# Another written-down order of the same operations, written-down buffer slots, and a small buffer for the last 160 tokens' piece of batch 3

## The chip, the cores and the metric

The kernel runs on one core of a Trainium2 chip. The metric is the device time of one execution in microseconds (us). The kernel before takes 217.79 us, the median of three runs (217.53 to 218.53).

A core has five engines, each with an instruction queue of its own that is worked off in order: TensorE (PE) multiplies matrices, VectorE (DVE), ScalarE (ACT) and GpSimd (POOL) work on vectors, and SyncE (SP) issues DMAs. ACT and POOL issue some DMAs too. In the profile, "PEld" is TensorE's loading of weights, "SPq" the DMA issue of SP. An engine waits for another's result on a semaphore.

## The reference

Polysketch attention, and then a token mixer on its output:

```python
# 4 batches, 4 heads, 1088 tokens, head size 32, r = 8
phi(x) = outer(S1 x, S2 x)                     # 64 features for each token
kv  = einsum('bhsf,bhsd->bhfd', phi(k), v)
z   = sum(phi(k), over s)
num = einsum('bhsf,bhfd->bhsd', phi(q), kv)
den = einsum('bhsf,bhf->bhs', phi(q), z) + 1e-6
x   = (num / den) as (batch, 1088, 4*32)

theta = x @ w_theta                            # 128x128
zr, zi = x * cos(theta), x * sin(theta)
y = w_tok_r @ zr + w_tok_i @ zi                # 1088x1088 each, over the tokens
u = x + y
out = u + relu(u @ w_ch)                       # 128x128
```

The weights come as 64-bit floats; the kernel itself turns the words of each weight into 32-bit floats.

## The kernel before, in words

**Recorded, then issued in a written order.** The kernel body computes nothing at first. Each call of `L.op(engine, duration, function, writes, reads)` in class `Layout` (L180) records one operation, with its engine ("P", "V", "A", "G", "S" for PE, DVE, ACT, POOL, SP), its buffers, and what it depends on. There are 1,020 operations. `L.run()` (L248) then walks the constant `ORDER` (L34), a permutation of their numbers, beside `STARTS`, a planned start for each in hundredths of a us. Each buffer has a class with a fixed number of slots; the first operation that touches a buffer gives it, of the free slots of its class, the one that falls free first by the planned times. `L.issue()` (L269) emits the operations in that order. Since each engine works its queue in order, `ORDER` decides what stands ahead of what on each engine, and which buffer's last use a slot has to wait for.

The classes (L344 and on) are `big` (22 slots of 1152 words for each partition: q, k, v, the converted token rows), `zs` (5 of 2176: raw token rows, turned x, z), `hf` (6 of 576), `g3` (5 of 768), `g1` (6 of 384), `sm` (13 of 192), `lv` (1) and `ps` (the 8 banks of PSUM).

**Fills.** Between two marked PE operations, `issue` also writes matmuls on a buffer of zeros (`spin`, L427, 128x384 in bf16) into PE's queue, as many as five for each planned microsecond of gap. Before them all stand 39 narrow ones (128x112). Their result is not read. There are 28 of the wide kind in the trace, one of them an operation of its own.

**Stages.** For each batch:

- `load` (L655): k, q and v, 576 KB each. k of batches 0 and 1 is issued by ACT, the rest by SP. q of batch 3 comes in four pieces of many small packets.
- key sums, grid and rests (L677 to L765) make the key features; for batches 1 to 3, `join` (L391) lets POOL issue a DMA that accumulates a correction into a second copy of k, loaded by SP at L714 ("kh" below is that copy).
- `kfeatures` (L767), `chain` (L835), `chain_out` (L933): transposes, features, the kv products, then small matrices that `levels` needs. Parts of them are POOL's (`blocks_m`, L569; masks, L379).
- `query_scale`, `query_slices` (L985, L1007), `levels` (L1033), `den` (L1059): the query features and the denominator.
- `outputs_x` (L1088): numerator, theta, sine and cosine, and the products zr and zi. For batches 1 to 3 x is transposed by a trip through DRAM: DVE transposes in blocks (L1160), SP stores it to the buffer `far` (L1161), four DMAs of SP fetch it (L1165).

**The token weights.** `weight` (L636) makes one row block of `w_tok` (there are 17, rows 0 to 16, each 1,088 KB for both w_tok_r and w_tok_i): SP loads it raw into a `zs` slot (L642), ACT converts the high words (L643) and the low words (L645), DVE shifts (L383) and adds (L379). The queue of SP, the two conversions of ACT and the two of DVE stand in order among all else that these engines do.

**The mixer.** For batches 0 and 1, `mix_row` (L1256) accumulates over the 17 row blocks in PSUM, batch 0 for three column groups together, batch 1 group by group. Batches 2 and 3 together use Winograd's seven products (`winograd`, L1352): each of m1 to m7 multiplies 544 tokens by 544 in two parts, 384 and 160 columns wide, and each result is added to u (`acc`, L1405). The number pair after "out" or "m" below is batch, half, part: out3_0_1 is batch 3's first half, the part 160 wide.

**The end.** When a piece of u is complete, `finish` (L1282) does its product with w_ch (PE), adds the relu (DVE, L386), transposes (DVE, L1303) and stores (L1299, by SP, ACT and POOL). For out3_0_1 `finish_turned` (L1329) does it in another way: PE transposes u (L1337), ACT copies that from PSUM (L1338) into `xT[3]`, the batch's own buffer, PE does the two products, DVE adds, SP and ACT store (L1347). The transposes, the copy and the products are one recorded operation.

Of the kernel before, what the change touches and what calls it, by code (L numbers as in the profile page):

```python
# [22 lines left out]
P = 128  # L23
# [11 lines left out]
    29, 32, 4, 2, 5, 0, 1, 3, 34, 30, 356, 50, 33, 102, 44, 96, 6, 108, 103, 36, 7, 51, 366, 54, 144, 8, 97, 10, 9,  # L35
    11, 55, 109, 20, 52, 12, 57, 139, 58, 59, 60, 61, 62, 63, 126, 13, 31, 132, 56, 98, 127, 264, 14, 391, 128, 143,
    245, 15, 145, 64, 65, 67, 68, 78, 35, 69, 16, 70, 19, 148, 149, 150, 151, 152, 268, 99, 66, 79, 246, 53, 80, 100,
    110, 129, 17, 133, 130, 357, 25, 361, 81, 270, 83, 18, 203, 358, 359, 71, 41, 153, 104, 271, 210, 197, 351, 257,
    45, 146, 72, 198, 73, 204, 247, 43, 258, 84, 26, 105, 360, 240, 74, 154, 323, 248, 214, 75, 82, 27, 325, 368, 106,
    155, 269, 28, 47, 76, 249, 111, 46, 77, 147, 386, 216, 85, 326, 86, 21, 327, 324, 87, 112, 205, 88, 328, 241, 89,  # L40
    120, 48, 242, 90, 206, 329, 121, 251, 367, 91, 330, 92, 134, 93, 101, 376, 392, 94, 122, 140, 252, 156, 107, 123,
    141, 369, 135, 259, 169, 142, 124, 95, 439, 436, 157, 22, 136, 362, 437, 115, 442, 217, 438, 443, 174, 440, 260,
    370, 444, 335, 441, 158, 159, 160, 161, 343, 363, 445, 265, 243, 170, 113, 446, 171, 371, 162, 352, 172, 215, 447,
    163, 164, 165, 166, 211, 39, 191, 167, 173, 448, 114, 168, 212, 175, 244, 449, 331, 176, 192, 177, 266, 450, 336,
    117, 37, 451, 341, 267, 332, 116, 253, 118, 452, 342, 339, 353, 178, 333, 272, 453, 193, 364, 340, 119, 199, 179,
    454, 125, 254, 462, 344, 387, 219, 131, 455, 137, 463, 200, 465, 180, 365, 464, 456, 181, 194, 466, 49, 458, 457,
    182, 469, 467, 459, 334, 183, 354, 460, 468, 337, 184, 470, 461, 472, 255, 138, 476, 381, 471, 473, 42, 185, 484,
    388, 474, 478, 396, 338, 273, 372, 220, 221, 274, 275, 250, 186, 40, 276, 222, 277, 256, 542, 479, 475, 539, 486,
    374, 492, 23, 373, 38, 487, 477, 195, 540, 494, 188, 480, 543, 495, 481, 355, 536, 482, 485, 218, 537, 544, 483,
    541, 278, 213, 279, 223, 280, 281, 283, 187, 224, 225, 284, 488, 226, 285, 227, 286, 287, 389, 288, 289, 290, 291,  # L50
    501, 489, 375, 538, 490, 378, 545, 502, 491, 292, 496, 261, 382, 546, 503, 498, 390, 393, 504, 547, 383, 401, 384,
    377, 548, 416, 394, 505, 549, 282, 398, 406, 379, 493, 550, 229, 380, 397, 230, 231, 262, 232, 233, 234, 235, 293,
    236, 385, 497, 237, 189, 426, 506, 304, 294, 551, 499, 238, 228, 302, 295, 552, 507, 296, 402, 303, 399, 553, 299,
    263, 403, 508, 395, 417, 418, 554, 500, 509, 555, 421, 408, 207, 558, 556, 201, 196, 239, 300, 400, 202, 301, 208,
    305, 562, 510, 559, 411, 209, 190, 557, 306, 569, 307, 560, 404, 407, 565, 308, 570, 405, 309, 561, 566, 572, 310,
    563, 345, 573, 311, 511, 564, 409, 312, 571, 313, 574, 346, 567, 314, 670, 568, 419, 676, 575, 579, 413, 316, 576,
    593, 580, 671, 412, 24, 581, 677, 577, 410, 673, 431, 678, 674, 582, 297, 586, 672, 414, 422, 512, 415, 594, 587,
    424, 578, 423, 513, 420, 427, 425, 514, 428, 429, 584, 595, 515, 583, 430, 596, 298, 675, 588, 320, 516, 679, 589,
    585, 590, 315, 598, 680, 591, 601, 624, 347, 647, 625, 681, 348, 648, 682, 649, 597, 592, 432, 626, 683, 602, 433,
    684, 603, 685, 627, 686, 604, 434, 650, 349, 317, 651, 599, 605, 687, 652, 435, 653, 654, 688, 655, 696, 628, 517,  # L60
    689, 703, 606, 350, 524, 741, 518, 738, 530, 318, 739, 690, 531, 742, 740, 319, 704, 735, 525, 743, 736, 697, 519,
    705, 737, 744, 607, 706, 745, 707, 608, 708, 709, 746, 629, 747, 656, 748, 630, 321, 749, 698, 750, 751, 609, 699,
    700, 752, 631, 701, 702, 322, 720, 753, 691, 761, 721, 754, 610, 692, 693, 657, 694, 853, 695, 632, 755, 611, 762,
    756, 722, 658, 710, 757, 758, 713, 759, 760, 763, 768, 711, 612, 764, 769, 714, 765, 659, 723, 715, 766, 782, 860,
    767, 770, 858, 775, 633, 771, 712, 772, 526, 773, 716, 774, 634, 776, 635, 789, 777, 613, 778, 660, 614, 790, 779,
    636, 717, 725, 615, 718, 780, 637, 783, 719, 616, 724, 520, 726, 727, 600, 661, 784, 728, 662, 729, 804, 781, 521,
    638, 791, 854, 813, 805, 796, 806, 797, 532, 785, 798, 792, 814, 527, 807, 730, 859, 794, 822, 786, 522, 815, 787,
    533, 816, 855, 823, 799, 793, 788, 663, 732, 639, 731, 850, 808, 800, 879, 640, 528, 861, 795, 529, 641, 832, 664,
    862, 851, 801, 833, 733, 834, 817, 523, 803, 818, 809, 857, 863, 856, 870, 534, 824, 802, 535, 944, 882, 835, 825,
    949, 948, 836, 871, 852, 819, 872, 883, 810, 884, 864, 909, 811, 865, 908, 866, 873, 874, 642, 867, 885, 875, 812,  # L70
    876, 911, 826, 820, 868, 665, 821, 890, 880, 887, 837, 838, 881, 617, 734, 891, 869, 618, 888, 899, 827, 886, 892,
    986, 900, 913, 839, 945, 840, 666, 893, 619, 894, 910, 901, 877, 946, 902, 889, 916, 952, 895, 878, 828, 829, 951,
    903, 917, 954, 904, 896, 918, 956, 897, 926, 912, 830, 919, 914, 831, 920, 898, 905, 947, 842, 953, 921, 843, 906,
    915, 927, 959, 907, 643, 958, 968, 969, 644, 922, 955, 667, 970, 841, 923, 845, 957, 960, 846, 961, 668, 950, 669,
    962, 645, 963, 971, 964, 965, 966, 972, 620, 967, 928, 985, 929, 621, 977, 844, 988, 987, 978, 989, 847, 622, 990,
    849, 848, 991, 623, 992, 973, 974, 975, 993, 646, 976, 994, 979, 930, 931, 980, 995, 981, 996, 924, 997, 998, 999,
    982, 925, 1000, 984, 983, 1008, 1001, 936, 1009, 1002, 1003, 937, 1004, 1005, 1010, 1006, 932, 1012, 1011, 933,
    1013, 1007, 934, 938, 1014, 935, 1015, 939, 1016, 1017, 1018, 940, 1019, 941, 942, 943,
)
STARTS = (  # L80
    73, 73, 90, 92, 103, 130, 170, 220, 358, 404, 449, 458, 493, 510, 538, 546, 566, 579, 580, 584, 594, 612, 628,
    666, 802, 678, 693, 694, 706, 716, 719, 732, 752, 771, 798, 811, 812, 813, 815, 817, 819, 821, 823, 838, 830, 944,
    871, 899, 904, 918, 957, 967, 1088, 998, 1026, 1061, 1064, 1066, 1111, 1113, 1115, 1129, 1129, 1408, 1142, 1145,
    1155, 1164, 1168, 1170, 1172, 1174, 1176, 1225, 1236, 1251, 1251, 1260, 1271, 1299, 1303, 1313, 1319, 1327, 1334,
    1390, 1418, 1439, 1550, 1477, 1505, 1527, 1550, 1562, 1579, 1585, 1612, 1716, 1671, 1686, 1687, 1689, 1749, 1858,
    1782, 1796, 1814, 1832, 1831, 1845, 1870, 1884, 2128, 1909, 1941, 1947, 1948, 1951, 1963, 2024, 2038, 2053, 2070,
    2073, 2103, 2093, 2101, 2129, 2138, 2153, 2179, 2272, 2187, 2240, 2248, 2261, 2278, 2293, 2293, 2304, 2414, 2348,
    2351, 2373, 2388, 2390, 2434, 2422, 2432, 2446, 2467, 2471, 2523, 2530, 2537, 2545, 2565, 2573, 2578, 2593, 2594,
    2616, 2651, 2655, 2668, 2678, 2691, 2706, 2765, 2786, 2779, 2785, 2805, 2831, 2894, 2895, 2926, 2928, 2934, 2949,
    2953, 2967, 2982, 2981, 3002, 3018, 3042, 3046, 3086, 3088, 3102, 3105, 3108, 3126, 3164, 3190, 3192, 3220, 3230,  # L90
    3267, 3296, 3319, 3321, 3342, 3360, 3390, 3410, 3417, 3424, 3430, 3450, 3437, 3451, 3483, 3488, 3498, 3530, 3516,
    3547, 3561, 3562, 3567, 3583, 3606, 3611, 3613, 3619, 3626, 3633, 3652, 3651, 3667, 3677, 3687, 3690, 3697, 3717,
    3714, 3727, 3732, 3739, 3756, 3754, 3776, 3806, 3815, 3817, 3833, 3852, 3844, 3866, 3866, 3868, 3881, 3884, 3899,
# [44 lines left out]
    21022, 21031, 21057, 21092, 21092, 21100, 21114, 21135, 21171, 21188,  # L138
)
WARM = 0  # L140
FILL = 5.0
LOAD_LEAD = 60.0
RAW_LEAD = 30.0
CHAINS = ((0,), (1,), (2, 3))
# [35 lines left out]
class Layout:  # L180
# [67 lines left out]
    def run(self):  # L248
        slots = {c: [[0.0, None] for _ in range(n)] for c, (n, _) in self.classes.items()}
        for b in self.bufs:  # L250
            b.left = len(b.ops)
# [52 lines left out]
def act(n):  # L304
    return 0.17 + 0.00083 * n
# [1238 lines left out]
```

## Time and profile before

| | |
|---|---|
| median of three runs | 217.79 us (217.53 to 218.53) |
| the profiled execution's span | 215.9 us, 1.9 below the median |
| granted TensorE clock | 1.00 in nearly every stretch |
| mean HBM traffic over the span | 157 GB/s |
| 128x384 fills; 128x112 spins | 28; 39 |
| token rows loaded | 17, 1,088 KB each |
| accumulating DMAs of POOL (L393) | issued at 21.78, 39.89 and 54.21 us |
| the kernel's first token-mix matmul row | starts at 57.2 us |

Times in the profile are microseconds from the start of the span. A group of instructions is given by its line, engine and operation, then "output<-inputs" by buffer name, then its shape, its busy time, and the idle time of that engine just before it with what ended it. The chain of waits goes back from the last instruction of the program, at each step to the thing that released it. A "share of DMA" above 1.00 means that all 16 DMA engines were busy for the whole stretch.

### The profile page before, as it was taken

How to read it: one execution, taken by the hardware profiler on the slowest of the kernel's cores; microseconds unless marked ns; L12 is line 12 of the kernel's file. 1: busy time of each engine (PE TensorE's matmuls, PEld its weight loads, DVE VectorE, ACT ScalarE, POOL GpSimd, SP SyncE). 2: the span in 40 equal slices, each digit the busy share in tenths (PEclk: the TensorE clock that was granted, in tenths of full speed). 3: DMA queues.
4: the chain of work that ended last, by engine and by line, in shares of the span. 5: the costliest groups of instructions: out<-in, count | busy, mean ns of one | idle time of the engine just before them, and what ended most of it. 6: DMA issues, size and time to landing. Idle time of an engine off the chain costs nothing.

```text
span 215.9 us, 5832 instructions
## 1 busy us (share of the span) xinstructions
PE 208.9 (97%) x2396; PEld 152.8 (71%) x2396; DVE 174.3 (81%) x343; ACT 114.5 (53%) x256; POOL 59.7 (28%) x105
## 2 busy tenths in 40 slices
PE   7899999999999999999999999999999999999992
PEld 7677798868866666866668666667677776666781
DVE  1799998999999998999999798885994747456263
ACT  4899989999998895798704233363810000000000
POOL 1272740306400000604004100000006489950403
PEclk9999999999999999999999999999999999999998
DMA  6999999995998993192002402424050420010735
GB/s 222 395 418 419 384 365 420 425 315 97 360 285 267 416 432 145 75 308 45 0 0 32 74 3 112 114 109 112 2 88 15 67 39 0 0 23 8 125 55 103
DMA packets 28046, 37.09 MB, mean 172 GB/s; under 512 B 20564, under 2 KB 23044, under 8 KB 25844
## 3 DMA queue, kind: packets, MB, share of 16 engines
q1 hardware_dynamic: 22868, 31.86, 42.4%
q0 software_dynamic: 1552, 3.25, 7.2%
q10 hardware_dynamic: 3600, 1.62, 2.8%
q8 instruction: 19, 0.31, 0.6%
q14 instruction: 7, 0.06, 0.1%
HBM read 29.84 MB, written 4.00 MB: 157 GB/s over the span
## 4 chain that ended last, share of the span: by engine, by line
PE 63%; DMA 18%; ACT 14%; issue 2%; SPq 1%; DVE 1%; POOL 1%; POOLq 0%; ACTq 0%
PE ps L399 61%; DMA zs<-w_tok 13%; DMA big<-k_l 5%; ACT big L645 4%; ACT big L643 3%; ACT lv L1056 1%; PE ps L1131 1%; ACT big L1021 1%; ACT g L1199 1%; ACT g L1202 1%; ACT g L1205 1%; ACT g L1203 1%; POOL out L1299 1%; SPq L671 0%; ACT g L1135 0%
## 5 line engine op out<-in xcount | busy, mean ns | idle before, releaser
L399 PE MATMUL ps<-big,zs 128*128 128x384 f32 (+2 forms) x380 | 110.5, 436 | 0.0
L399 PEld LDWEIGHTS ps<-big,zs 128*128 128x128 f32 x380 | 66.9, 190 | 32.5
L379 POOL TENSOR_TENSOR big<-big,big 128x544 f32<-128x544 f32 x16 | 22.1, 1458 | 48.6 <-DVE big L379 44.6
L399 PE MATMUL ps<-big,big 128*32 128x32 f32 (+2 forms) x352 | 22.8, 234 | 0.0
L643 ACT ACTIVATE big<-zs 128x1088 f32<-128x1088 f32 x17 | 20.9, 1231 | 1.5 <-DMA zs<-w_tok 0.9
L379 DVE CUSTOM_DVE_ANT_0 big<-big,big 128x2176 uint16<-128x2176 uint16 x17 | 21.5, 1275 | 0.0
L645 ACT ACTIVATE big<-zs 128x1088 int32<-128x1088 uint32 (+1 forms) x18 | 21.4, 1194 | 0.3 <-DMA zs<-w_tok 0.3
L1338 ACT COPY big<-ps 80x256 f32<-80x256 f32 x1 | 0.4, 368 | 39.6 <-DMA out<-g 39.6
L399 PEld LDWEIGHTS ps<-big,big 128*32 128x32 f32 (+1 forms) x352 | 15.3, 124 | 6.8 <-issue 0.8
L1276 ACT COPY g<-ps 128x384 f32<-128x384 f32 (+1 forms) x6 | 2.5, 466 | 23.4 <-PE ps L399 23.4
L379 DVE TENSOR_TENSOR big<-big 128x544 f32<-128x544 f32 x8 | 9.5, 1204 | 5.6 <-PE ps L399 5.6
L383 DVE TENSOR_SCALAR big<-big 128x1088 int32<-128x1088 int32 x17 | 12.2, 719 | 0.0
L379 POOL TENSOR_TENSOR mf<-mv,sm 128x32 f32<-128x32 f16 (+1 forms) x3 | 0.8, 262 | 39.1 <-DVE sm L379 39.1
L428 PE MATMUL ps<-idle 128*128 128x112 bf16 (+1 forms) x67 | 10.0, 312 | 1.3 <-POOL idle L430 1.3
L379 DVE TENSOR_TENSOR g<-lv 128x768 f32<-128x768 f32 x12 | 11.1, 950 | 0.1
L399 PEld LDWEIGHTS ps<-w,big 128*128 128x128 f32 (+1 forms) x76 | 9.8, 189 | 1.4
L379 DVE TENSOR_TENSOR big<-big,hf 128x1152 f32<-128x1152 f32 x8 | 10.7, 1351 | 0.0
L399 PE MATMUL ps<-w,big 128*128 128x128 f32 (+1 forms) x76 | 10.5, 278 | 0.0
L399 PE MATMUL ps<-sbk,g 128*128 128x64 f32 x72 | 10.0, 276 | 0.3 <-ACT g L793 0.3
L379 DVE TENSOR_TENSOR zs<-zs,g 128x384 f32<-128x384 f32 (+2 forms) x24 | 9.8, 447 | 0.2
L386 DVE SCALAR_TENSOR_TENSOR big<-ps,even,big 128x384 f32<-128x384 f32 (+1 forms) x10 | 4.8, 493 | 6.3 <-PE ps L399 6.2
L1199 ACT ACTIVATE g<-ps 128x384 f32<-128x384 f32 x12 | 5.9, 504 | 7.3 <-PE ps L399 7.3
(199 smaller groups left out, 379.2 us busy)
## 6 DMA issues: line engine op xcount, KB each, us to landing
zs<-w_tok SPq DMA_DIRECT2D x17, 1088.0 KB, 10.6
big<-k_l SPq DMA_DIRECT2D x5, 576.0 KB, 13.2
big<-v_l SPq DMA_DIRECT2D x4, 576.0 KB, 15.6
big<-q_l SPq DMA_DIRECT2D x3, 576.0 KB, 10.7
big<-hf POOLq DMA_DIRECT2D x3, 576.0 KB, 10.0
far<-zs SPq DMA_DIRECT2D x3, 576.0 KB, 2.8
zs<-far SPq DMA_DIRECT2D x12, 144.0 KB, 4.3
big<-k_l ACTq DMA_DIRECT2D x2, 576.0 KB, 4.4
```

Source lines behind the costliest of these rows:

```text
L379: eng.tensor_tensor(out=o, in0=a, in1=b, op=f)
L383: (eng or V).tensor_scalar(out=o, in0=a, scalar1=s1, scalar2=s2, op0=op0, **kw)
L386: (eng or V).scalar_tensor_tensor(out=o, in0=a, scalar=s, in1=b, op0=op0, op1=op1)
L399: T.matmul(o, lhs, rhs, start=start, stop=stop, skip_group_check=True)
L428: T.matmul(nowhere()[:, :n], idle()[:, 0:P], idle()[:, :n], start=True, stop=True, skip_group_check=True)
L643: op("A", 0.22 + n * 0.0009, lambda: A.activation(dfn(), words_of(raw(), n)[1].bitcast(F32), AF.Prelu, scale=2.0**-112, alpha=-(2.0**32)), ...
L645: op("A", 0.22 + n * 0.0009, lambda: A.activation(stp(), words_of(raw(), n)[0].bitcast(U32), AF.Copy, scale=2.0**-29), [stp], [raw])
L1021: op("A", act(GW) + 0.1, lambda g=g, tr=tr: A.activation(f()[:, g * GW:(g + 1) * GW], tr(), AF.Copy, scale=s()[:, 0:1]), [(f, g)], [tr, (s ...
L1056: op("A", act(480), lambda g=g, lp=lp: A.copy(lv().rearrange("p l (c n) -> p l c n", n=HR)[:, :, g * GC:(g + 1) * GC], lp().rearrange("p c ...
L1131: T.transpose(tr()[:, i * P:(i + 1) * P], qp()[:, i * H + 2 * n:i * H + 2 * n + 2].rearrange("p h i j -> p (h i j)"), ident())
L1199: op("A", act(GW), lambda cs=cs, th=th: A.activation(cs()[:, 0], th(), AF.Copy, bias=ROUND), [(cs, 0)], [th])
L1276: op("A", act(w), lambda: A.copy(u(), yp()[:, :w]), [uT], [yp])
```

## The change

Four things change in the text of the kernel.

1. `ORDER` is another permutation of the same operations. It has 1,021 numbers, since `finish_turned` records one more.
2. `STARTS` is gone, and with it the choice of slots at run time. A constant `SLOTS` gives each buffer its slot.
3. The planned gaps are gone. A constant `GAPS` says before which five operations fills stand, 9 in all.
4. `finish_turned` writes to a buffer of its own, `yb`, of class `g1`, in place of `xT[3]`. Its transposes, the copy and the products are recorded as three operations (PE, ACT, PE), and the relu's add is sized by the 256 columns it has. An empty DVE operation goes.

The number of PE instructions falls by the fills; DVE's, ACT's, POOL's and SP's work is the same, in another order. The order on each engine differs from before nearly everywhere.

```diff
-ORDER = (
-    29, 32, 4, 2, 5, 0, 1, 3, 34, 30, 356, 50, 33, 102, 44, 96, 6, 108, 103, 36, 7, 51, 366, 54, 144, 8, 97, 10, 9,
...
+ORDER = (
+    0, 4, 29, 32, 2, 1, 96, 5, 102, 50, 54, 120, 55, 57, 58, 59, 60, 97, 6, 33, 34, 61, 108, 144, 30, 139, 62, 140,
...
-STARTS = (
-    73, 73, 90, 92, 103, 130, 170, 220, 358, 404, 449, 458, 493, 510, 538, 546, 566, 579, 580, 584, 594, 612, 628,
...
+GAPS = {57: 2, 67: 3, 14: 2, 90: 1, 257: 1}
+SLOTS = (
+    0, 1, 3, 6, 2, 0, 6, 9, 1, 3, 4, 8, 12, 0, 16, 5, 17, 0, 19, 0, 0, 2, 7, 4, 4, 9, 15, 2, 4, 10, 11, 4, 0, 1, 4, 6,
...
-FILL = 5.0
...
     def run(self):
-        slots = {c: [[0.0, None] for _ in range(n)] for c, (n, _) in self.classes.items()}
...
         self.order = [self.ops[i] for i in ORDER]
...
-                    free = [(s[0], i) for i, s in enumerate(slots[b.cls]) if s[1] is None]
-                    b.slot = min(free)[1]
...
+        for b, slot in zip([b for b in self.bufs if b.cls is not None], SLOTS):
+            b.slot = slot
+
+    def issue(self, pools, fill):
         for o in self.order:
-            if o.eng == "P":
-                if on:
-                    for _ in range(int((o.start - last - 0.08) * FILL)):
-                        fill()
-                last, on = o.end, on and o is not span[1] or o is span[0]
+            for _ in range(GAPS.get(o.i, 0)):
+                fill()
...
     def finish_turned(b, t0, w, u, keys, due):
...
-        y = lambda: xT[b]()[:n, 0:2 * DM]
+        yb = buf("g1", (2 * DM,), F32, "yb")
+        y = lambda: yb()[:n]
+
+        def turned():
+            for c in range(2):
+                T.transpose(pu()[:n, c * DM:(c + 1) * DM], u()[:, c * n:(c + 1) * n], ident())
...
-            A.copy(y(), pu()[:n, 0:2 * DM])
...
-        op("P", w * 4 / 2400 + 0.01, products, [po, pu], keys + [w2])
-        vop(w, lambda: stt(y(), po()[:n, 0:2 * DM], 0.0, y(), ALU.max, ALU.add), keys, [po])
-        vop(w, lambda: None, [], keys)
+        op("P", 0.2, turned, [pu], keys, hold=[yb])
+        op("A", act(2 * DM), lambda: A.copy(y(), pu()[:n, 0:2 * DM]), [yb], [pu])
+        op("P", 0.35, products, [po], keys + [w2])
+        vop(2 * DM, lambda: stt(y(), po()[:n, 0:2 * DM], 0.0, y(), ALU.max, ALU.add), [yb], [po])
...
-        op("S", w * P * 2 / 100e3, lambda: store(SY, 0), [], keys, due, lk=2)
-        op("A", 0.92, lambda: store(A, 1), [], keys, due, fly=2.1)
+        op("S", w * P * 2 / 100e3, lambda: store(SY, 0), [], [yb], due, lk=2)
+        op("A", 0.92, lambda: store(A, 1), [], [yb], due, fly=2.1)
```

Read off the new order, on the engines that the prediction speaks of: SP's queue of loads is k2, k3, the second copy of k1, q0, q1, w_sq, v0, the second copies of k2 and k3, q2, row 5, v1, row 9, row 3, a piece of q3, row 0, row 1, a piece of q3, row 2, v2, row 4, the last pieces of q3 with batch 1's store to DRAM between them, batch 1's fetches, row 6, v3 and rows 8, 11, 7, 10, 13, 12, 14, 16, 15. In before it was k3, q0, row 1, k2, w_sq, q2, row 3, the second copy of k1, v0, row 8, q1, row 2, v1, row 0, v3, the second copy of k3, row 7, and so on. The last of Winograd's products in after's order is m3's part of 384 columns for batch 3's first half (operation 924); in before it was m3's part of 160 (934).

## The prediction

> **What bounds the kernel now.** Read the busy times first, then the stretches of ten microseconds, then the chain of waits, then the end of the timeline. The busy times name TensorE:
>
> ```profile
> PE 208.9 (97%) x2396; PEld 152.8 (71%) x2396; DVE 174.3 (81%) x343; ACT 114.5 (53%) x256; POOL 59.7 (28%) x105
> PE 63%; DMA 18%; ACT 14%; issue 2%; SPq 1%; DVE 1%; POOL 1%; POOLq 0%; ACTq 0%
> ```
>
> The 97% is not what it seems. The ends of matmuls are modelled, so a matmul that is issued and then waits counts as busy, and fills (matmuls on the buffer `idle`) count too. I therefore took start-to-start distances where PE runs densely: 0.65 us for two 128x384 f32 matmuls, 0.27 for two 128x160, 0.163 for a bf16 fill. With these, PE has 194.5 us of work up to its last instruction. What I call the **delay** of an instruction is its start less the sum of all work ahead of it on its engine. At PE's end the delay is 16.5 us: 1.3 start, 4.6 fills, the rest waits. It is 3.9 at 9 us, 10.5 at 30, 13.2 at 50, 15.2 at 100, 16.5 at the end. So four fifths of what an order can win lies in the first 50 us.
>
> There, two other things are as full as PE (columns: PE, PEld, DVE, ACT and POOL busy, granted clock, DMA share, GB/s):
>
> ```profile
> 10.00:20.00 10.00, 9.74 (x204) 7.88 (x203) 9.62 (x20) 9.87 (x26) 4.86 (x17) 1.00 1.02 417
> 20.00:30.00 10.00, 9.97 (x198) 7.91 (x197) 9.62 (x27) 9.30 (x27) 4.64 (x12) 1.00 1.02 373
> 30.00:40.00 10.00, 9.87 (x220) 8.93 (x221) 9.34 (x19) 9.33 (x27) 3.11 (x13) 1.00 1.02 418
> 40.00:50.00 10.00, 9.75 (x142) 7.68 (x142) 9.66 (x24) 9.43 (x23) 0.84 (x2) 1.00 1.02 328
> 170.00:200.00 30.00, 30.00 (x123) 20.41 (x122) 17.82 (x32) 0.48 (x1) 18.30 (x15) 1.00 0.11 18
> ```
>
> DVE and ACT are at 93 to 99% and the DMA engines saturated until 50 us. After 100 us PE alone sets the time (one chain link of 86.46 us on PE), until the end:
>
> ```profile
> 208.50 2.34 PE L399 MATMUL ps<-big,zs 128*128 128x160 f32 x16
> 210.06 0.32 DVE L379 TENSOR_TENSOR big<-big,ps 128x160 f32<-128x160 f32 x1 [0.32 <-PE ps L399]
> 210.68 0.43 PE L399 MATMUL ps<-big,w 128*128 128x160 f32 x2
> 211.17 1.81 POOL L1299 DMA_DIRECT2D out<-g  x3 [0.50 <-DVE g L1303]
> 211.77 0.37 ACT L1338 COPY big<-ps 80x256 f32<-80x256 f32 x1 [39.55 <-DMA out<-g]
> 212.79 0.40 SPq L1347 DMA_DIRECT2D out<-big  x1
> ```
>
> From 210.68, where PE is next free, to the span's end at 215.9 it is 5.2 us, with 0.9 us of PE work in it. The span lies 1.9 us under the median of 217.79; that I keep.
>
> **The change part by part.** The operations are the same but for the number of fills, so everything lies in who waits for whom. I wrote both orders engine by engine and summed before's durations ahead of each instruction.
>
> *DVE against PE (gain).* Where a PE instruction reads a DVE result, compare the work ahead of each. In before the worst is the conversion of token row 8: 69.7 us of DVE work ahead of it, against 64.0 us of PE work ahead of its reader, an excess of 5.7 us; several others are over 5. In after no excess is above 0.6. DVE also begins with batch 0's keys, and its first delay falls from about 6 to about 4.9. Were this all, PE's delay would fall to about 10: a gain of up to 6.5.
>
> *DMA order (loss).* After's queue on SP is k2, k3, the second copy of k1, q0, q1, the small weight, v0, the second copies of k2 and k3, q2, row 5, v1, rows 9, 3, a piece of q3, rows 0, 1, a piece of q3, row 2. Prices from landings of before: 576 KB take 1.5 us of a saturated DMA, one 1,088 KB token row 2.63 (landings 76.94 and 79.58), and an accumulating copy of POOL (section 6: 10.0 us from issue to landing) about 2.1, because row 2 landed 4.8 us behind q1 instead of 2.6 while one ran. In before these three copies are issued at 21.78, 39.89 and 54.21; in after all three can go within the first 23 us. Row 2 in after: 12 loads x 1.5 + 0.6 + 6 rows x 2.63 + two q3 pieces at some 1.4 (an estimate, from landings around 52 us) = 37.2, from a start at 3.0: about 40; with three copies 46.5. ACT meets row 2 with 33.8 us of work ahead of it, so its delay there is 6 or 13, against 8.2 in before at 50 us. Row 5 and row 9 give the same picture (10.5, and 7 or 13). ACT's results go to DVE with slack of only 0.3 to 1.5, and DVE's to PE with none. On POOL the second and third copies now stand ahead of batch 0's matrices for the level stage, which come near 26.7 instead of 22.8. I take the joins as costing what the one row shows: PE's delay at 50 us then is 13.5 to 14, as before (13.2). The order's gain is eaten.
>
> *After 50 us.* Row loads come late to ACT (delay up to 16), with 4 to 11 us of slack to DVE: nothing. The trip of batch 1's x through DRAM lasted 9.7 us in before (7.6 and 8.4 for the other two batches), and DVE had 10.0 us of other work beside it; after has 6.9, so DVE waits 0.7 to 2.8 us there. PE in before lost 2.8 more from 50 to the end; I give after 2.3: delay 16.0 against 16.5, **-0.5**. Bounds: -6.5 (nothing of DMA binds) and +1.5 (copies, trip and lock step all bind).
>
> *Tail (loss).* In after the last mixing product is 128x384 wide, not 128x160. Behind it stand its sum 0.55, the channel product 0.81, the relu-and-add 0.56, the transpose 0.57 (rows of the same width earlier in the tail) and hand-overs of about 0.6: 3.1. Then POOL issues two stores and, in order, one that was ready before: 0.3, then 2 x 0.6 (issues at 211.17, 211.77, 212.38), landing 2.0 (section 6, `out<-g` POOLq of 20 KB), and 1.14 from the last landing (214.76) to the close: 7.7 in all. PE work left is 1.6 instead of 0.9. So 7.7 - 5.2 - 0.7 = **+1.9**. Bounds: +1.2 if the third store is gone by then, +2.3 if stores contend.
>
> *Fills, slots, the small buffer.* 9 fills fewer than 27 stand where PE waits anyway: 18 x 0.163 = 2.9 us if each were on the path, and I put 0, since the DVE excess ends the waits they lie in. The written slots add waits for buffers only where a reader is late; by the summed orders these are under 0.3. `finish_turned` with a buffer of its own spares ACT's copy a wait (39.55 us idle ahead of it), but its issue is behind the matmuls anyway: 0. Its split into three operations lets PE's products pass the copy: 0 to -0.2.
>
> A rule that speaks against the change, apart from the sum: the granted clock reads 1.00 in every stretch, and the 39 first fills, 112 wide, run 93 ns apart, while the later 384-wide ones take 163 ns. "TensorE: Matmul & The Clock Gate" in the Trainium skill says under "What's actually happening" that an idle window of about 3.4 us halves the clock and as much activity restores it. The row agrees with half rate at the start (112 columns in 93 ns is 1.2 per ns); no row of before shows a second cold stretch.
>
> Sum: 215.9 - 0.5 + 1.9 = 217.3 for the span, with 1.9 around it **219.2 us**.
>
> **The rivals.**
> - *Faster: the DMA hides.* If copies take no DMA time from loads, row 2 lands at 40, ACT's delay is 7 to 8 and PE's about 10: -6.5 + 1.9 = -4.6, 213.2 us. For it: only one pair of landings prices a copy, and after shows no excess of DVE. Against: a saturated DMA until 50 us. It decides at a row 2 landing under about 43.
> - *Same: half of it.* Waits bind at one place only, or the engines' orders differ on paper while the waits stay the same (the change doesn't do what it says): PE's delay 14.3, -2.2 + 1.9, 217.5.
> - *Slower still: a cold or lock-stepped PE.* PE is unfilled for up to 5 us near 22 to 27. If the clock drops there, the next 3.4 us, as long as PE took to speed up at the start, do half their work: 1.7 us, 220.9. Against: short gaps with work between. The same page would give this time by its rule.
>
> **How the numbers follow.** Forecast 0.42 (217.9 to 220.5), the DMA hides 0.31 (212 to 216), same 0.17, cold 0.10. 0.5%, 1.09 us, is about what a measurement of this kernel can tell from no change. Faster: 0.31 and a little of "same", 0.34. Same: the rest of it and the forecast's low edge, 0.17. Slower: 0.49. Range 212.7 to 221.6: from the hiding rival less a little to cold plus the tail's bound.
>
> **What would show it.** Right: row 2 landing near 46.5 and ACT waiting for `w_tok` ahead of its step; PE's first token-mix row (57.2 in before) not earlier than 56; DVE waiting 1 to 3 us at batch 1's turned x; the last mixing product 384 wide, and 7 to 8 us from there to the end. Wrong: copies landing in the first 23 us with loads 2.6 apart around them; the first mix row at 52 or before; a granted clock under 1.00 between 20 and 35 us; a tail near 5 us.

## The result, and the profile after

The changed kernel takes 241.56 us (median of four executions, 240.67 to 242.19) against 217.66 beside it: a ratio of 1.107, 95% interval 1.102 to 1.111. The forecast was 219.2, at most 221.6. Its sign was right, its size was not: +24 us instead of +1.4. Executions of this order differ more from each other than those of the order before (238.1 to 247.9 on another chip), for a reason that the traces show below; medians here are of all executions, ratios of the undisturbed ones alone.

First the page of the changed kernel: busy times, the granted clock in 40 slices of 6 us, and the chain's shares.

```profile
span 240.4 us, 5808 instructions
PE 222.0 (92%) x2378; PEld 162.3 (68%) x2378; DVE 178.7 (74%) x343; ACT 117.9 (49%) x257; POOL 64.4 (27%) x105
PEclk9975557769999999999999999999999999999996
PE 63%; DVE 12%; ACT 8%; DMA 8%; issue 4%; SPq 2%; POOL 1%; POOLq 0%; DVEq 0%; ACTq 0%
```

The clock falls in the third slice. Then the stretches (PE, PEld, DVE, ACT, POOL busy, clock, DMA share, GB/s), beside those shown of before:

```profile
10.00:20.00 10.00, 6.05 (x132) 5.03 (x121) 3.81 (x15) 4.15 (x16) 3.54 (x11) 0.73 1.04 369
20.00:30.00 10.00, 10.00 (x120) 9.21 (x118) 6.03 (x13) 5.92 (x17) 5.31 (x20) 0.50 1.02 415
30.00:40.00 10.00, 10.00 (x204) 9.26 (x204) 7.51 (x15) 6.22 (x18) 6.42 (x22) 0.58 1.09 328
40.00:50.00 10.00, 10.00 (x174) 9.01 (x177) 7.02 (x21) 6.82 (x20) 0.45 (x2) 0.77 0.84 283
180.00:200.00 20.00, 20.00 (x82) 13.32 (x80) 19.07 (x29) 0.48 (x1) 10.89 (x8) 1.00 0.17 28
```

DVE and ACT, 93 to 99% busy there before, are now at 38 to 75%. PE is not: it is slow. Its records show where that begins (start, duration, idle time before and what ended it):

```profile
11.24 0.20 PE L334 MATMUL ps<-big 128*32 128x32 f32 x1
15.38 0.27 PE L334 MATMUL ps<-big 128*32 128x32 f32 x3 [3.95 <-issue]
```

PE stands still for 4.1 us in the middle of one recorded operation (74, a piece of batch 0's key sums), between two matmuls with the same operands. "issue" says that the profile knows of nothing it waited for. At 14.59 the clock goes to half, and stays there until 38.48, and again from 45.31 to 52.14: 30.7 us in all. The end, last:

```profile
230.54 0.31 DVE L314 TENSOR_TENSOR big<-big,ps 128x160 f32<-128x160 f32 x1
232.18 0.62 DVE L321 SCALAR_TENSOR_TENSOR big<-ps,even,big 128x384 f32<-128x384 f32 x1 [1.32 <-PE ps L334]
232.90 0.86 PE L334 MATMUL ps<-big,w 128*128 128x384 f32 x2
234.39 0.58 DVE L1238 STREAM_TRANSPOSE g<-big 128x384 f32<-128x384 f32 x1
235.26 1.81 POOL L1234 DMA_DIRECT2D out<-g  x3 [4.84 <-DVE g L1238]
```

It is as forecast: a 384-wide product last, its sum, channel product, add and transpose behind it, and three stores of POOL.

**Where the time is.** With the same sums of work as in the prediction, PE's delay at one and the same operation (456, the transposes that open batch 0's numerator; the expectations below call it the first numerator product) is 27.6 us, and 12.6 in before: **+15.0**. From there to PE's end it grows by 10.8 instead of 3.9: **+7**. From PE's last mixing product to the close it is 8.4 us instead of 5.2, with 0.7 more of PE's work in it: **+2.5**. Together 24.5, the difference of the spans.

### The profile page after: what moved, and what is told of

It is laid out like the page before. It is cut to its first block, busy times and chain, and to the rows that moved or that the text cites. A ratio compares the mean times of both kernels' runs of the same rounds, so it can differ in the third digit from the quotient of the medians.

```text
span 240.4 us, 5808 instructions
## 1 busy us (share of the span) xinstructions
PE 222.0 (92%) x2378; PEld 162.3 (68%) x2378; DVE 178.7 (74%) x343; ACT 117.9 (49%) x257; POOL 64.4 (27%) x105
## 4 chain that ended last, share of the span: by engine, by line
PE 63%; DVE 12%; ACT 8%; DMA 8%; issue 4%; SPq 2%; POOL 1%; POOLq 0%; DVEq 0%; ACTq 0%
PE ps L334 55%; DVE big L314 5%; DVE zs L314 3%; DMA far<-zs 3%; DMA zs<-far 3%; PE ps L725 2%; PE ps L953 2%; DMA big<-k_l 2%; SPq L1100 2%; ACT big L578 1%; ACT g L1070 1%; DVE zs L1095 1%; PE ps L1066 1%; PE ps L363 1%; ACT big L1079 1%
## 5 line engine op out<-in xcount | busy, mean ns | idle before, releaser
L334 PEld LDWEIGHTS ps<-big,zs 128*128 128x128 f32 x380 | 65.9, 190 | 32.9 <-DVE big L314 1.0
L314 POOL TENSOR_TENSOR big<-big,big 128x544 f32<-128x544 f32 x16 | 23.6, 1500 | 22.1 <-DVE big L314 22.0
L334 PEld LDWEIGHTS ps<-big,big 128*32 128x32 f32 (+1 forms) x352 | 15.7, 139 | 10.3 <-issue 2.6
L328 POOL DMA_DIRECT2D g<-big x6 | 5.3, 1036 | 56.5 <-ACT g L1211 51.9
L334 PE MATMUL ps<-sbk,g 128*128 128x64 f32 x72 | 13.9, 359 | 0.0
L334 PEld LDWEIGHTS ps<-sbk,g 128*128 128x128 f32 x72 | 13.2, 273 | 0.2
L314 DVE TENSOR_TENSOR big<-big,hf 128x1152 f32<-128x1152 f32 x8 | 10.8, 1356 | 0.0
L321 DVE SCALAR_TENSOR_TENSOR big<-ps,big 128x384 f32<-128x384 f32 (+1 forms) x7 | 3.1, 444 | 9.4 <-PE ps L334 9.3
L1234 POOL DMA_DIRECT2D out<-g x8 | 5.0, 632 | 18.8 <-DVE g L1238 18.8
L334 PEld LDWEIGHTS <-hf 128*32 128x32 bf16 (+1 forms) x252 | 7.7, 101 | 3.4 <-issue 1.4
## 6 DMA issues: line engine op xcount, KB each, us to landing
big<-q_l SPq DMA_DIRECT2D x3, 576.0 KB, 10.2
big<-hf POOLq DMA_DIRECT2D x3, 576.0 KB, 10.2
```

The lines of the kernel that those rows point to most:

```text
L314: eng.tensor_tensor(out=o, in0=a, in1=b, op=f)
L321: (eng or V).scalar_tensor_tensor(out=o, in0=a, scalar=s, in1=b, op0=op0, op1=op1)
L328: op("G", 0.9, lambda: G.dma_start(dst(), src(), accum_op=ALU.add), w, r, fly=fly)
L334: T.matmul(o, lhs, rhs, start=start, stop=stop, skip_group_check=True)
L1234: E.dma_start(out[b, s0:s0 + n, f * SQ:(f + 1) * SQ].rearrange("(c j) i -> j c i", j=SQ), ot()[f * SQ:(f + 1) * SQ, :n].rearrange("j (c i) ...
```

## The experiments

The theories: **A**, PE had used up the instructions that it holds, and the next ones had not come. **B**, the operation in which it stopped waited for something of its own. **C**, the fills, 9 instead of 27, let the clock fall. For A, the trace has the packets of the instruction queue among its DMA records (the page's queue list: 19 packets, 0.31 MB, so 16 KB each), and PE's records can be counted (its matmuls, its weight loads and the semaphore instructions that the trace has between them): it stopped behind record 449.

**24 fills ahead of operation 70.**

```diff
-GAPS = {57: 2, 67: 3, 14: 2, 90: 1, 257: 1}
+GAPS = {57: 2, 67: 3, 70: 24, 14: 2, 90: 1, 257: 1}
```

> The changed kernel with 24 fills of 384 columns (3.9 us of matmuls that nobody reads) ahead of the fourth of the key-rest operations. Theory A (TensorE has used up the instructions it holds at record 449, counting matmuls and weight loads, the next 16 KB packet of instructions has not come, and the idle time of 4.1 us then drops the clock): the packet still comes near 12.9 and PE goes on near 15.4, but it is busy until 14 or so, so the idle time is under 1.5 us, the granted clock stays at 1.00, and the kernel becomes faster than the changed one by 8 us or more (under 233), although it has more work. Theory B (the operation in which PE stops waits for its own data or bank): the stop stays as it is or moves by the 3.9 us, the clock falls, time 241 to 245. Theory C (too few fills are what lets the clock fall, whatever the stop): the clock stays up as in A, but PE still stops at the same operation.

238.95 us, ratio 1.091 (1.086 to 1.096): 3.9 us of idle matmuls made it a little faster. The stop at 449 and the fall of the clock at 15 us are gone, but PE stops elsewhere:

```profile
21.93 0.22 PE L334 MATMUL ps<-hf 128*32 128x32 bf16 x6 [1.26 <-issue]
35.33 3.94 PE L334 MATMUL ps<-mf,big 128*128 128x96 f32 x17 [3.42 <-issue]
```

These stops are behind records 705 and 1217, which is 449 + 256 and 449 + 3 x 256. The clock falls at 34.66, within the second, for 17.1 us. The gain of over 8 us was not reached, since the loss only moved.

**The same work, later.** Operations 70 to 75 behind 104.

```diff
-    ... 132, 70, 71, 72, 73, 141, 12, 147, 74, 75, 214, 83, 264, 13, 14, 15, 98, 99, 104, 251, ...
+    ... 132, 141, 12, 147, 214, 83, 264, 13, 14, 15, 98, 99, 104, 70, 71, 72, 73, 74, 75, 251, ...
```

> The changed kernel with six of the key-rest operations of batch 0 (70 to 75) written behind operations 14, 98 and 104 (the scaling of the sketch and two feature products); no fill is added and no work is changed. Theory A: PE comes to record 449 at about 13.7 instead of 11.2, and goes on at about 15.4, an idle time of 1 to 2 us, the clock stays at 1.00 or dips for one short stretch, and the time falls to 222 to 232. Theory B (data or bank of operation 74): the stop stays at operation 74 with 4 us or disappears. Theory C (fills): the clock falls as before, 238 to 242.

240.26 us, ratio 1.099 (1.096 to 1.102). PE comes to record 449 at 13.94 and stops for 2.4 us, now with its packet at 13.96; at 705 it stops again, for 1.0. The clock falls all the same, for 27.3 us. So the place is as A says, and the time is not: a stop of 2.4 us is enough for the clock.

**Fewer records ahead.**

```diff
-    op("P", 3.2, lambda: [spin(112) for _ in range(39)], [nowhere], [idle], due=-10.0)
+    op("P", 3.2, lambda: [spin(336) for _ in range(13)], [nowhere], [idle], due=-10.0)
```

> The changed kernel with 13 first spins of 336 columns instead of 39 of 112: the same columns, 52 records fewer. Theory A: PE stops at the same count of records, 449, so 52 records later in the code, inside operation 14 or 98 and no longer in operation 74, for 3 to 4.5 us; the clock falls as before; time within 3 us of the changed kernel. Theory B: PE stops in operation 74 still. Theory C says nothing of the place.

238.49 us, ratio 1.088 (1.081 to 1.094). PE runs through operation 74 without a pause and stops 52 records later in the code, ahead of the feature product 98, again behind record 449, for 3.4 us; and for 2.8 behind 961. **B falls.** The profile names a releaser here, POOL's `sq`, but the run above did the same product straight behind operation 14 with no such wait: it is what happened to end near.

**The DMA engines empty.** SP stores two words of batch 0's grid first:

```diff
+            if o.i == 144:
+                hold()
             o.fn()
...
-        L.issue(pools, spin)
+        seen = hop.tile([P, 2], F32, tag="seen", name="seen")
+        L.issue(pools, spin, lambda: SY.dma_start(seen, kg[0]()[:, 0:2]))
```

(The eight loads from 144 on are written behind operation 52.)

> The changed kernel with SP held back: ahead of the second copy of k1 it stores two words of batch 0's grid, which are ready at about 9.7 us, so that all later loads come some 6 us later, and the DMA engines run empty at about 10. Theory A1 (the packet with PE's next instructions waits behind data packets, 3.8 us in the changed kernel from where PE enters its last held part at 9.1): the packet starts before 11, PE goes on before 13.5, and the stop at record 449 is 2.3 us or less. Theory A2 (the packet is as late whatever the DMA engines do): it starts at 12.5 to 13 and the stop stays at 4. The time itself: 236 to 246, since the loads come late too.

```profile
11.05 0.20 PE L336 MATMUL ps<-big 128*32 128x32 f32 x1
12.47 0.23 PE L336 MATMUL ps<-big 128*32 128x32 f32 x3 [1.22 <-issue]
```

The packet starts at 10.3 instead of 12.87, and the stop at record 449 lasts 1.4 us instead of 4.1: **A1 holds**, instructions queue behind data. The whole is 241.88 us (ratio 1.096, 1.089 to 1.107): PE waits for the late loads at 17.1 instead, and the clock falls there.

**The kernel before without fills.** `FILL = 0.0`.

> The kernel before without its 27 wide fills (one is left that is an operation of its own). Theory A: what matters is whether PE reaches record 449 before about 15.1; in the kernel before it passes there at 15.72 with 0.6 us to spare, and the fills ahead of it are 20 to 50 records, so an idle stretch of at most 1 to 2 us; the clock holds, time within 2.5 us of before. Theory C: the clock falls between 15 and 40 us as in the changed kernel, and the time rises by 8 us or more.

231.86 us, ratio 1.063 (1.059 to 1.068). PE stops at the end of no block before 80 us, and yet:

```profile
10.00:20.00 10.00, 9.95 (x152) 8.69 (x150) 8.75 (x18) 8.93 (x23) 3.88 (x17) 0.54 1.02 417
20.00:30.00 10.00, 9.87 (x154) 8.68 (x153) 7.62 (x18) 7.01 (x22) 4.41 (x11) 0.50 1.02 394
```

The clock is at half from 10.76 to 41.48, and again for 6.8 us from 89.26, with a stop of 2.7 us behind record 2753. The fills that I priced at 2.9 us at most hold up 13.5 us of the kernel before. My expectation (A alone) was wrong here, **C holds for the clock**.

**More fills in the changed kernel**, 24 ahead of 70 and 12 ahead of 158 and of 439.

> The changed kernel with 24 fills ahead of operation 70 as in the first run, and 12 more ahead of operation 158 and 12 ahead of 439 (7.8 us of fills in all added). Theory A and C together (PE is held up where it has used its instructions, at records 449, 705, 961, 1217 and so on, and an idle stretch with too few fills halves the clock): no stop of over 3 us is left before 40 us, the clock holds at 1.00 until 60 us, and the time falls to 226 to 235 in spite of the fills. If the half clock cost little, the time stays at 238 to 245 with the clock at 1.00.

243.23 us, ratio 1.112 (1.103 to 1.121). The clock is full until 40.6 and at half for 10.2 us only; the stops left are 0.9 and 1.7 us. Against the changed kernel's trace the half clock is 20.5 us shorter, which is up to 10.2 us of work, and the stops are 1.5 us shorter; but the 48 fills are 7.8 us of PE's own time, and operation 456 starts at 58.5 instead of 59.7. In the median nothing is gained.

**One part of the change at a time.** The kernel before with the nine fills of the changed one:

```diff
-FILL = 5.0
+GAPS = {57: 2, 67: 3, 14: 2, 90: 1, 257: 1}
...
-            if o.eng == "P":
-                if on:
-                    for _ in range(int((o.start - last - 0.08) * FILL)):
-                        fill()
-                last, on = o.end, on and o is not span[1] or o is span[0]
+            for _ in range(GAPS.get(o.i, 0)):
+                fill()
```

> The kernel before, its order and slots, with the changed kernel's nine fills (ahead of the same five operations) in place of its own 27: one part of the change alone. Theory C (the clock halves when a stretch of 3.41 us has too little of PE's work and comes back only after a nearly full one; the order before needs its fills): the clock falls somewhere between 10 and 40 us, 222 to 233. If the nine stand where they are needed, the clock holds and the time is 216 to 219, and then the fills alone do not explain the change.

229.48 us (225.29 to 231.23), ratio 1.039 (1.031 to 1.047). In the profiled execution PE stops at a block's end once, behind record 1985, for 1.0 us. The clock holds until 22.24 and is at half for 17.1 us:

```profile
20.00:30.00 10.00, 9.57 (x131) 8.54 (x130) 7.95 (x18) 7.87 (x23) 4.42 (x11) 0.61 1.03 378
30.00:40.00 10.00, 10.00 (x110) 9.52 (x111) 6.90 (x14) 5.39 (x14) 3.91 (x8) 0.53 1.03 420
```

The changed kernel with the 27 fills of before:

```diff
-GAPS = {57: 2, 67: 3, 14: 2, 90: 1, 257: 1}
+GAPS = {11: 3, 57: 3, 79: 3, 110: 1, 203: 8, 153: 1, 77: 5, 86: 2, 163: 1}
```

> The changed kernel with the 27 fills of the kernel before, ahead of the same operations as there, in place of its nine: that part of the change undone. Theory A: eleven of 14 records more stand ahead of record 449, so PE still stops there at 11 to 12 us for 3 us or more, and the clock falls all the same in the stretch of that stop; the later fills shorten the half-clock time. 234 to 242. Theory C alone (the fills, not the stop): the clock holds and the time falls under 232.

241.78 us (238.00 to 248.79), ratio 1.098 (1.089 to 1.107). In the profiled execution, of 248.79 us, the stop at 449 stays (3.8 us), one at 1217 comes (2.7), and the clock is at half for 34.1 us: fills that stand behind a late block come late with it. The executions of 238.00 and 241.16 us had mean clocks of 0.976 and 0.971, against 0.928 in the changed kernel, so the fills do lift the clock in some executions; what held the time up in those two, no trace shows.

Both repairs, these fills and 70 to 75 behind 104:

> The changed kernel with both repairs together: operations 70 to 75 behind 14, 98 and 104, and the 27 fills of the kernel before. Theory A and C together: the stop at record 449 is 1 to 2.5 us, the fills hold PE's activity up, the half-clock time is under 20 us (31 in the changed kernel), and the time is 228 to 238. If the early part is not what costs, 240 or more.

238.04 us, ratio 1.089 (1.084 to 1.093). No stop at 449, half clock for 10.2 us, and stops of 1.9 and 1.6 us behind 1217 and 1473. The changed kernel once more, beside these three:

> The changed kernel once more, beside the three above on the same chip, as their measure: 238 to 246, with the stop at record 449 for 3.5 to 4.5 us and 27 to 31 us of half clock.

Median 242.96. Its fastest execution, 238.14 us, had the highest mean clock (0.948), its slowest, 247.88, the lowest (0.913). On the medians of this chip both repairs together are worth 4.9 us, but that fastest execution is as fast as the median with both. In the profiled executions operation 456 starts at 56.0 with both and at 59.7 in the first trace of the changed kernel. By either measure the repairs return a third of the early 15 or less.

The early part as a whole can be checked by a sum, an estimate from the traces. Operation 456 starts at 44.1 in before. Add 0.163 for each wide fill more than before's (subtract it for each fewer), half of the time at half clock, the stops at the ends of blocks, and 0.6 for the other work that the new order puts ahead of it. The sum gives 61.3 for the changed kernel (59.7 measured), 59.4 with 24 fills (59.7), 54.7 with fewer records (55.0), 57.4 with 48 fills (58.5), 49.7 for the order of before with nine fills (50.6). Over the 17 traces in which the clock falls ahead of it, operation 456 starts anywhere from 50.6 to 67.1; the sum is within 1.5 us of it in 11 and within 3.4 in all. It misses most with both repairs (53.3 against 56.0) and where the half clock is longest (68.1 against 64.8). So the half clock and the late blocks account for the early loss, but for some 3 us either way.

**Behind 60 us.** Trips through DRAM that wait for nothing (batches 2 and 3 get batch 1's x):

```diff
+            hops.append(far)
-            def fetch():
+            def fetch(far=hops[0]):
```

> The changed kernel with the fetches of batch 2's and batch 3's turned x reading what batch 1 stored, so that they wait for no store; batches 2 and 3 are mixed with wrong data, all instructions and bytes stay. Theory D (between 150 and 200 us the two trips through DRAM, one behind the other, set DVE's start and so PE's): 3 to 4.5 us less than the changed kernel, 237 to 238.5. Theory E (DVE's own order and load set it there, and the trips are hidden): within 1 us of it, 240.5 to 242.

243.32 us (240.28 to 245.57). Since the early clock moves these totals, I read a stretch that it does not reach: from operation 456 to 918 (a product of m3) the changed kernel takes 153.6 us, this one 152.5. Ten more traces that leave this stretch as it is take 153.3 to 154.7 for it, so the total alone would hardly show 1 us; PE's wait behind the trip, below, does. The trips are worth 1 us, not 3 to 4.5.

DVE's row conversion on half of the columns, in both kernels:

```diff
+        m = n // 2
-        ... ts(dfn().bitcast(I32), dfn().bitcast(I32), 3, ALU.logical_shift_left)
+        ... ts(dfn()[:, :m].bitcast(I32), dfn()[:, :m].bitcast(I32), 3, ALU.logical_shift_left)
-        ... tt(V, dfn().bitcast(I32), dfn().bitcast(I32), stp(), ALU.add)
+        ... tt(V, dfn()[:, :m].bitcast(I32), dfn()[:, :m].bitcast(I32), stp()[:, :m], ALU.add)
```

> The changed kernel with DVE's two operations on each token row done on half of its columns (the other half of the weights stays unconverted and the mixing is wrong); 17 rows, half of 1.28 and 0.72 us each, so 17 us of DVE's work gone, most of it between 60 and 130 us. Theory F (behind 60 us DVE sets the pace of the changed kernel, since its order leaves DVE more work for then: DVE is busy 9.3 to 9.97 of 10 us there and PE's delay grows by 10 us): 5 to 9 us less than the changed kernel, 232 to 237, with PE's growth of delay from 60 us to the end down to 1 to 5 us. Theory G (ACT, a transfer or PE itself): 239 to 243.

244.52 us (237.03 to 248.41), and 152.9 for the stretch: F falls. DVE loses 17 us of work and PE wins 0.7.

> The kernel before with the same half conversion, the control of the run above. PE has the pace behind 60 us (9.95 to 10.0 of 10 us); only the waits for DVE ahead of 60 us can go: 1 to 4 us less than before, 214 to 217, unless PE reaches a record 449 + 256 k too early and stops there. By theory G for the changed kernel nothing is said of this one.

218.31 us, ratio 1.0005 (0.998 to 1.003). Operation 456 starts at 43.3 instead of 44.1, but at 77.9 PE stops for 1.5 us:

```profile
78.08 1.18 ACT L645 ACTIVATE big<-zs 128x1088 int32<-128x1088 uint32 x1 [0.29 <-DMA zs<-w_tok]
79.39 0.25 PE L399 MATMUL ps<-sq,sm 32*32 32x16 f32 x8 [1.28 <-ACT sm L851]
```

That is near the end of a block (record 2752; 449 + 9 x 256 is 2753), but the block's packet had been in since 72.0. PE waits for a copy of ACT, which stands behind the conversion of a token row that landed at 78.0 (76.94 in before). What DVE gives, a transfer takes back. The 1 to 4 us that I expected were not there to be had.

With half of ACT's second conversion left out too, and with the trips as well:

> The changed kernel with half of each token row left out in DVE's two operations and in ACT's second one (the weights are wrong), 17 us of DVE's and some 10 us of ACT's work less, mostly between 60 and 130 us. What is read is the stretch from the start of operation 456 (the first numerator product of batch 0) to operation 918 (a product of m3), 153.6 us in the changed kernel and 152.8 with DVE's half alone; the early clock does not reach into it. Theory H (ACT sets the pace between 60 and 90 us, busy 9.6 to 9.96 of 10 us there, and DVE takes over): 147 to 151. Theory I (DVE's and ACT's load does not matter, PE waits for single results that the order has put just ahead of it): 152 to 154.

> The same, and the fetches of batch 2's and batch 3's turned x read what batch 1 stored, as in the run on the trips. Theory H: 145 to 150, some 1 to 2 less than the run without. Theory I: 151.5 to 153.5, one less by the trip alone, as the 152.6 of the run on the trips.

245.03 and 241.69 us (two executions each); the stretch takes 154.8 (1.6 of it at a short fall of the clock near 208) and 152.1. H falls too, and I is what is left. PE's waits in the stretch, in the changed kernel, are for single results:

```profile
80.53 0.55 PE L1124 MATMUL ps<-ident,big 128*128 128x128 f32 x3 [1.09 <-ACT big L1079]
91.36 1.88 PE L334 MATMUL ps<-big,zs 128*128 128x384 f32 x5 [0.47 <-DVE zs L314]
179.13 0.78 PE L334 MATMUL ps<-big,big 128*128 128x160 f32 x4 [1.53 <-DVE big L314]
201.00 1.18 PE L334 MATMUL ps<-big,big 128*128 128x384 f32 x4 [0.99 <-DVE big L314]
203.01 0.54 PE L334 MATMUL ps<-big,w 128*128 128x160 f32 x2 [0.82 <-DVE big L314]
```

They are 4.9 of the 10.8 us; in before PE has none there but one of 0.2. They come at the same operations in every variant, except that the second is gone with DVE's half alone. With the trips free, the third is 0.55 to 0.60 instead of 1.53: that is the 1 us of the trips. In the written order the last four results stand 1 to 8 places ahead of their readers, the first 60. Before's growth of 3.9 comes without such waits, so some 2 of the +7 stay open.

**The end, and the small buffer.** First only the last 46 operations, then the last 49 written so that no 384-wide piece comes last:

> The changed kernel with only the end written in another order: the last four products of 384 columns for batch 3's first half come ahead of the last three of 160, and their piece's channel product, sum, transpose and stores with them, so that the 160-wide piece is last, as in the kernel before. By the prediction's tail term: 5.2 to 5.8 us from the last product to the close instead of 7.5, and 1.3 to 2.2 us less than the changed kernel (239.4 to 240.3). If the end is set by stores alone, no change.

243.23 us (239.45 to 247.99). PE waited 1.4 us for a sum that I had put just ahead of its product, so nothing came of it.

> The changed kernel with its last 60 operations written anew: the remaining products of 384 columns for batch 3's first half come ahead of the last ones of m4 and of the 160 columns, so that no long piece is left and PE need not wait for a sum. By the prediction's tail term: 1.2 to 2.2 us less from PE's last mixing product to the close, and from the whole; since the times of the changed kernel vary by some us with the clock early on, the stretch from 220 us on in the trace decides: the close comes 9.5 to 10.5 us behind the end of the fifth of m4's 384-wide products, against 12.5 in the changed kernel.

244.60 us, ratio 1.111 (1.106 to 1.116). The count of 12.5 in this expectation was wrong: from the end of m4's last 384-wide product to the close the changed kernel takes 14.3 us. Here it is 13.8. From the last mixing product to the close it is 7.3 instead of 8.4, but PE comes to that product 0.6 later, so 0.5 of the tail's 2.5 us came back.

> The kernel before with only the small buffer of its own for the last 160 tokens' piece of batch 3's first half; the order, the slots' rule and the fills stay. The prediction put it at 0: 217.3 to 218.7, no difference from before. If the copy into that batch's own buffer held something up, up to 1 us less.

218.26 us, ratio 1.000 (0.998 to 1.003). The new buffer alone does nothing, as forecast.

## Why the prediction was wrong

- **The step that failed: PE's delay, "13.5 to 14, as before" at 50 us and 16.0 at the end.** It was 27.6 at operation 456 and 38.4 at the end. The sum let PE wait for engines and transfers only, with its instructions always there and its clock always full; what a cold PE costs stood outside it, as a rival of 1.7 us. Half clock for 30.7 us is up to 15.4 us of work not done, and the stop at record 449 is 4.1; less the 2.9 us of 18 fills that are gone, this is 16.6 against +15.0 measured.
- **What bounds the kernel.** The sums of work were fit for what they count, but two things that PE needs are in no engine's queue: its instructions and its clock. Before 50 us the kernel before already runs close to the pace of the first: from record 193 (9.98 us) to 1473 (41.81) it is 6.4 us for each 256 records, and where PE stopped it was 5.6 to 8.0 us, once 8.6, from the entry of one block to the use of the next while the DMA engines were saturated. At record 449 it had 0.7 us to spare (packet in at 13.56, about 1.5 more until its use, passed at 15.72).
- **DVE against PE, "a gain of up to 6.5".** PE did come earlier: 9.09 instead of 9.98 at record 193. But a PE that is earlier only meets the block that is not there. The rival "the DMA hides" with its 213.2 us did not come either: its sign was row 2 landing under 43.
- **"Fills ... I put 0".** Wrong too, without a reason that held. Cut to nine in the order of before, they cost some 8.5 us (ratio 1.031 to 1.047); cut to none, 13.5. My cover ("stand where PE waits anyway") is why they matter: they keep PE active in its waits. But in the new order the 27 fills alone brought the median from 242.96 to 241.78 only, so there the late blocks come first.
- **"Slower still: a cold or lock-stepped PE", 1.7 us, chance 0.10.** The half clock was named, but not its place, its cause or its length. I looked for it in a stretch without fills near 22 to 27 us; it came at 14.59, in the stop for instructions. I let the clock come back after 3.4 us; it came back after 23.9. I had also read the clock of before as 1.00 in every stretch; from 200 to 215.9 it is 0.93, since it falls at 213.8. PE was done by then, so this cost nothing.
- **"DMA order (loss)".** Row 2 landed at 49.0 (46.5 forecast), but ACT did not wait for it: its step started at 62.3, since PE held ACT up. The copies were issued at 12.14, 27.67 and 28.33, not all in the first 23 us. The 13.5 to 14 us of delay at 50 us were 24.
- **After 50 us, "delay 16.0".** 2.3 us of growth were forecast; from operation 456 on 10.8 came, 3.9 in before. The trips through DRAM are 1 us of it. At batch 1's turned x, the place that I named, DVE waited 1.25 us, as forecast (0.7 to 2.8). My argument that ACT's and DVE's slack hides late rows stands (leaving out their work changes nothing); what I took for a gain, DVE's results at most 0.6 us late by the sums, leaves no slack, and PE waits at a handful of them.
- **Tail.** +1.9 forecast (7.7 - 5.2 - 0.7 is 1.8), +2.5 measured (8.4 from the last mixing product to the close; 7.7 forecast). Right in its steps, 0.6 to 0.7 short.
- **Small buffer.** 0, measured 0.
- **The signs.** One sign of being wrong came: a granted clock under 1.00 between 20 and 35 us. PE's first token-mix row began at 85.2, so "not earlier than 56" held, but for another reason.

## What to carry to other kernels

Count TensorE's instructions as a load of its own: with saturated DMA engines a block of 256 took some 6 us and more to come here, and a burst of small matmuls outran it. A stop "from issue" at a fixed stride of records is its mark; check that the packet had not been in long before. Idle matmuls in waits were not waste here, and the price of taking them away was the clock's fall, so price that by the thinnest 3.4 us stretch. An order that looks better by queue sums has to be paced against both before its sums mean anything.

## What the runs showed of the hardware

- **Instruction blocks.** PE's stops at this stride (behind records 449, 705, 961, 1217, 1473, 1985 or 2753, of 0.9 to 5.0 us) occur in 17 of the 20 traces, whatever operation stands there. At these stops the packet starts 3.2 to 6.3 us after PE enters the block before it, with the DMA engines saturated (share 0.89 to 1.12), and 1.4 with them nearly empty (0.03); it lasts 0.9 to 1.2, once 1.5, and PE goes on 1.2 to 1.8 later. The Trainium skill, "Runtime: NRT & Kernel Launch", section "Instruction fetch mechanics", gives blocks of 16 KiB and 256 instructions; the records agree. It calls their cost mostly hidden; here it is up to 5.0 us a time.
- **The clock's windows.** Changes come at multiples of 3.41 us. PE's activity can be worked out for each window: the columns of a matmul, twice for f32, at 384 in 0.16 us (a fill at full clock) or in 0.32 at half. From 7 us to PE's last matmul in the 20 traces, 30 of 31 falls followed a window at 0.38 or less and one a window at 0.42; the thinnest window that kept the full clock had 0.37. All 31 returns followed one at 0.73 or more, and windows at half clock up to 0.76 did not return. In the kernel before the thinnest window ahead of its end has 0.44 with its fills, and 0.36 without. So the fall needs no idle window, and the return needs a nearly full one. The Trainium skill, "TensorE: Matmul & The Clock Gate", section "What's actually happening", speaks of an idle window and a busy one of about 3.4 us; the length agrees, the two shares are measured here. The windows begin at another point of the kernel in each execution. The changed kernel was at half clock for 30.7 us ahead of its end in one profiled execution and 41.0 in another; half of the difference is 5.1 us, and the two spans differ by 5.6. That is the spread above.
